# Windowed attention and SwiGLU on one core: the second token group loaded in token order

## The chip, the cores and the metric

The kernel runs on one core of a Trainium2 chip. The core has five engines that run side by side: TensorE (matrix products; weight loads and products are listed apart as PEld and PE), VectorE (DVE), ScalarE (ACT), GpSimd (POOL) and SyncE (SP). Data come from HBM by DMA, over 16 transfer engines that all queues share. The metric is the device time of one execution in microseconds (us), median of several.

## The reference

It is an attention over a sliding window with sink tokens, followed by a gated feed-forward block. There are 4 sequences of 768 tokens, 8 heads of 64.

```python
scores = scale * np.matmul(q, k.transpose(0, 1, 3, 2))
is_sink = pos[None, :] < n_sink                  # 4 sink tokens
rel = pos[:, None] - pos[None, :]
in_window = (rel >= 0) & (rel < window)          # window of 128
scores = np.where(is_sink | in_window, scores, -1e9)
a = np.exp(scores - scores.max(-1, keepdims=True))
a = a / (a.sum(-1, keepdims=True) + 1e-09)
attn = np.matmul(a, v)
# ... heads side by side: x is (3072, 512)
g = x @ w_gate                                   # 512 x 1536
val = x @ w_val
out = (g * sigmoid(g) * val) @ w_out             # 1536 x 512
```

## The kernel before: the parts that matter

The tokens are cut into 12 groups of 256 (3 to a sequence). For each group the kernel loads k, q and v, turns k and q so that the head dimension lies on the partitions, computes scores, exponentials, masks, values and normalization, turns the result (xn) into xT, and hands it to the gate, value and down projections. These are slices of matmuls ("units") in whose gaps the attention of later groups is woven. The order on every engine is the order of the program.

Group 0 is loaded first, in a form of its own. Group 1 is loaded by rows: each partition gets four tokens of one head in one piece of 256 numbers, and 64 small matmuls against an identity turn it. Groups 2 and 3 are loaded in token order (a partition is a token, its heads are pieces of 64 numbers) and turned by full 128x128 transposes.

```python
def load_rows(g, i):                       # i: k or q; two issues, one per half of the heads
    for w in range(2):
        nc.gpsimd.dma_start(rows[g][64 * w:64 * (w + 1), i],
                            by_rows((k, q)[i], b, w, ALL, c * 256))

def load_nat(g):                           # token order; k and q, two issues each
    # ...
    for i, src in ((0, k), (1, q)):
        for j in range(2):
            nc.gpsimd.dma_start(x[:, i, j].rearrange("p (h d) -> p h d", d=D),
                                src[b, :, t0:t0 + P].rearrange("h p d -> p h d"))

def step_T(g, i, p2, evict=None):          # turns rows: 16 matmuls of 64x64 and a copy
    # ...
def step_TN(g, i, j, evict="av"):          # turns token order: 4 transposes of 128x128
    pt = bank([P, NP2, P], BF16, "pn")
    for p in range(NP2):
        nc.tensor.transpose(pt[:, p], nats[g][:, i, j, p * P:(p + 1) * P], ident)
    # ... one copy out of PSUM, on ScalarE ("a") or VectorE ("v")
```

The loads on GpSimd's queue come in this order at the start: k and q of group 0 (heads 4 to 7; the others go over other queues), k and q of group 1, v of group 0, gate piece 0 (w_gate and w_val, 256 columns each), v of group 1, gate pieces 1 and 2; then group 2 and further weights.

The opening after group 0's scores:

```python
fill(14, bank([P, 512], FP32, "w"))        # matmuls on zeros, 256 columns, at the very start
# ... group 0: casts, turning, scores, masks
step_T(1, 0, 0, "a")
step_T(1, 0, 1, "a")
step_ks(0)                                 # the sinks' keys
step_T(1, 1, 0, "a")
step_T(1, 1, 1, "a")
step_PV(0, 0, 0)                           # values of group 0: (group, token half, head half)
step_PV(0, 0, 1)
flush()                                    # VectorE: normalization that was put off
step_PV(0, 1, 0)
step_PV(0, 1, 1)
flush()
step_S(1, 0)                               # scores of group 1, heads 0 to 3
masks1 = list(later)
later.clear()
step_K(1)                                  # scores against the sinks
step_X(0, 0, "now")                        # xn of group 0 turned into xT
step_X(0, 1, "now")
step_S(1, 1)                               # scores of group 1, heads 4 to 7
later[:0] = masks1
flush()
```

After it come the units. The first holds gate and value slices 0 and 1 of group 0 (`gate_held`); then `gate_first` computes the values of group 1 and starts gate slices 2 and 3, which need gate piece 1:

```python
us = [(gate_held, *g0[0][1:]), (gate_first, *g0[1][1:]), g1[0], g1[1], g0[2], g1[2],
      *((gate, "01", f) for f in range(6, DFC)),   # groups 0 and 1 joined: 512 columns
      *g2, *downs(0), *downs(1), *downs(2)]

def gate_first(tb, f, attn):
    for j, hh, norm in ((0, 0, "v"), (1, 0, "v"), (0, 1, "a"), (1, 1, "v")):
        step_PV(1, j, hh, norm)            # norm: "a" scales on ScalarE, "v" on VectorE
        flush()
    a = gate_a(tb, f)
    step_X(1, 0, "a")                      # copy on ScalarE
    step_X(1, 1, "now")                    # copy on VectorE
    held.pop()()
    gate_b(tb, f, *a)
```

A unit of one group, such as `g0[2]`, does two slices of the hidden dimension for 256 tokens; a joined unit ("01") does one slice for 512 tokens.

Of the kernel before, what the change touches and what calls it, by code (L numbers as in the profile page):

```python
# [7 lines left out]
FP32 = mybir.dt.float32  # L8
BF16 = mybir.dt.bfloat16
# [5 lines left out]
def kernel(  # L15
# [62 lines left out]
    def bank(shape, dtype, name):  # L78
        return psum.tile(shape, dtype, tag="b", name=name)


    rows, nats, vas = {}, {}, {}

    def by_rows(src, b, w, pairs, t0):

        hs = slice(2 * pairs.start + w, 2 * pairs.stop, 2)
        return src[b, hs, t0:t0 + 256].rearrange("p (m r) d -> m p (r d)", r=4)

    ALL = slice(0, NP2)

    def new_rows(g):
        rows[g] = rowp.tile([P, 2, NP2, 4 * D], BF16, tag="rows", name="rows")
        return rows[g]

    def load_rows(g, i):
        b, c = divmod(g, GC)
        if g not in rows:
            new_rows(g)
        for w in range(2):
            nc.gpsimd.dma_start(  # L100
                rows[g][64 * w:64 * (w + 1), i],
                by_rows((k, q)[i], b, w, ALL, c * 256))

    def load_nat(g):
        b, c = divmod(g, GC)
        x = (natp if g > 3 else rowp).tile(
            [P, 2, 2, DM], BF16, tag="nat" if g > 3 else "rows", name="nat")
        for i, src in ((0, k), (1, q)):
            for j in range(2):
                t0 = c * 256 + j * P  # L110
                nc.gpsimd.dma_start(  # L111
                    x[:, i, j].rearrange("p (h d) -> p h d", d=D),
                    src[b, :, t0:t0 + P].rearrange("h p d -> p h d"))
        nats[g] = x
# [37 lines left out]
    th8 = const.tile([P, 4, 4], FP32)  # L152
    lt8 = const.tile([P, 4, 4], FP32)
    sk = const.tile([P, 1], FP32)
    zero = const.tile([P, 256], BF16)
    one = const.tile([P, 1], FP32)
    warmed = const.tile([P, 1], FP32)
    KW = 32
# [28 lines left out]
    for i in range(2):  # L187
# [2 lines left out]
                   allow_small_or_imprecise_dtypes=True)  # L190
    nc.gpsimd.iota(tk, [[0, 1]], base=0, channel_multiplier=1,
                   allow_small_or_imprecise_dtypes=True)
    load_rows(1, 0)
    load_rows(1, 1)
    load_v(0)
    nc.gpsimd.iota(th8, [[-32, 4], [-NS, 4]], base=0, channel_multiplier=1,
                   allow_small_or_imprecise_dtypes=True)
# [12 lines left out]
    def flush():  # L210
        for f in later:
            f()
        later.clear()

    def new_T(b):
        if b not in kTs:
            kTs[b] = kqtp.tile([P, NP2, S], BF16, tag="kT", name="kT")
            qTs[b] = kqtp.tile([P, NP2, S], BF16, tag="qT", name="qT")

    def step_T(g, i, p2, evict=None):  # L220
        b, c = divmod(g, GC)
        new_T(b)
        x = rows[g]
        pt = bank([P, 2, 256], FP32, "pt")
        for pp in range(2):
            p = 2 * p2 + pp
            for r in range(4):
                for w in range(2):
                    h = slice(64 * w, 64 * (w + 1))
                    nc.tensor.matmul(  # L230
                        pt[h, pp, r:256:4], x[h, i, p, r * D:(r + 1) * D],
                        ident[h, h], start=True, stop=True, skip_group_check=True)
        dst = (kTs, qTs)[i][b][:, 2 * p2:2 * p2 + 2, c * 256:(c + 1) * 256]
        if (evict or ("a", "v")[i]) == "a":
            nc.scalar.copy(out=dst, in_=pt)
        else:
            nc.vector.tensor_copy(out=dst, in_=pt)

    def step_TN(g, i, j, evict="av"):

# [67 lines left out]
    def step_K(g):  # L308
        b, c = divmod(g, GC)
        if c == 0:  # L310
            return
        ps = bank([P, P], FP32, "pk")
        kfl = kss.rearrange("q b p x -> q b (p x)")
        for a in range(2):
            for j in range(2):
                for hh in range(2):
                    r, p = 32 * (2 * j + hh), 2 * hh + a
                    t0 = c * 256 + j * P
                    k0 = (KW + 2 * NS) * p - 2 * NS * a
                    nc.tensor.matmul(  # L320
                        ps[r:r + KW], kfl[:, b, k0:k0 + KW], qTs[b][:, p, t0:t0 + P],
                        start=(a == 0), stop=(a == 1), skip_group_check=True)
        es_t[g] = espool.tile([P, P], BF16, tag="es", name="es")
        nc.scalar.activation(es_t[g], ps, AF.Exp, scale=scale)
# [54 lines left out]
    def step_X(g, j, evict="v"):  # L379
        t0 = g * 256 + j * P  # L380
        tb = max(i for i in range(len(SIZES)) if OFF[i] <= t0)
        off = t0 - OFF[tb]
        if tb == 0 and off == 0:
            xTs["01"] = xtp.tile([P, DMC, 512], BF16, tag="xT", name="xT")
            xTs[0], xTs[1] = (xTs["01"][:, :, 256 * i:256 * (i + 1)] for i in range(2))
        elif tb > 1 and off == 0:
            xTs[tb] = dense(xtp.tile([P, DMC * 512], BF16, tag="xT", name="xT"),
                            DMC, SIZES[tb])
        if g not in PEX:
            def sp():  # L390
                nc.sync.dma_start_transpose(xTs[tb][:, :, off:off + P], xns[g, j])
            later.append(sp)
            return
        pt = bank([P, DMC, P], BF16, "px")
        for i in range(DMC):
            nc.tensor.transpose(pt[:, i], xns[g, j][:, i * P:(i + 1) * P], ident)  # L396

        if evict == "a":
            nc.scalar.copy(out=xTs[tb][:, :, off:off + P], in_=pt)
            return  # L400

        def dve():
            nc.vector.tensor_copy(out=xTs[tb][:, :, off:off + P], in_=pt)
        if evict == "now":
            dve()
        else:
            later.append(dve)
# [59 lines left out]

    def gate_first(tb, f, attn):

        for j, hh, norm in ((0, 0, "v"), (1, 0, "v"), (0, 1, "a"), (1, 1, "v")):  # L470
            step_PV(1, j, hh, norm)
            flush()
        a = gate_a(tb, f)
        step_X(1, 0, "a")
        step_X(1, 1, "now")
        held.pop()()
        gate_b(tb, f, *a)
# [62 lines left out]
    def fill(n, ps, cols=256):  # L540
        for _ in range(n):
            nc.tensor.matmul(ps[:, 0:cols], zero[:, 0:P], zero[:, 0:cols], start=True,
                             stop=True, skip_group_check=True)
# [40 lines left out]
        m = mask0.rearrange("q (o a) x -> q o (a x)", o=1)[:, :, P:512]  # L584
        nc.vector.tensor_tensor(e, e, m.broadcast_to([P, 2, 384]), op=ALU.mult)

    fill(14, bank([P, 512], FP32, "w"))
    cast(0, 0)
    cast(1, 0)
    nc.vector.tensor_scalar(mask[:, :, 0:P], tq2, tk, None, op0=ALU.is_lt)  # L590
# [28 lines left out]
    for i in range(4):  # L619
# [4 lines left out]
    nc.gpsimd.memset(vcl[:, :, D:D + 1], 1.0)  # L624
    load_sinks(vcl, 1, B)

    step_T(1, 0, 0, "a")
    step_T(1, 0, 1, "a")
    step_ks(0)
    step_T(1, 1, 0, "a")  # L630
    step_T(1, 1, 1, "a")
    step_PV(0, 0, 0)
    step_PV(0, 0, 1)
    flush()
    step_PV(0, 1, 0)
    step_PV(0, 1, 1)
    flush()
    step_S(1, 0)
    masks1 = list(later)
    later.clear()  # L640
    step_K(1)
    step_X(0, 0, "now")
    step_X(0, 1, "now")
    step_S(1, 1)
    later[:0] = masks1
    flush()

    g0, g1, g2 = gates(0), gates(1), gates(2)
    us = [(gate_held, *g0[0][1:]), (gate_first, *g0[1][1:]), g1[0], g1[1], g0[2], g1[2],
          *((gate, "01", f) for f in range(6, DFC)),  # L650
          *g2, *downs(0), *downs(1), *downs(2)]

    def L(*fs):
# [76 lines left out]
```

## Time and profile before

| what | value |
|---|---|
| time, median of 3 | 238.78 us (238.61 to 238.98) |
| span of the profiled execution | 237.8 us |
| TensorE busy | 229.1 us, 96% of the span |
| VectorE, ScalarE, GpSimd busy | 158.4, 113.7, 74.5 us |
| TensorE clock granted | full in every slice |
| gate and value matmuls (pg, pv) | 73.1 us each |
| down matmuls (pd) | 64.8 us |
| data moved by DMA | 27.36 MB in 107,655 packets |

The page gives busy time by engine; the chain that ended last tells what released what, back from the end; a timeline lists the instructions of an engine in order, with its idle time before them and what ended it in brackets. In the names, `pg<-xT,wg` is a matmul that writes tile pg from xT and the weights wg. L417 is the line of both projections, L100 the row loads, L122 the loads of v, L133 those of w_gate and w_val.

### The profile page before, as it was taken

The page shows a single profiled execution, that of the slowest core. Times are in us where ns is not written, and L with a number is a line of the kernel's source. Part 1 is how long each engine was busy: PE and PEld are TensorE (multiplying, and loading weights), DVE is VectorE, ACT ScalarE, POOL GpSimd, SP SyncE. Part 2 cuts the span into 40 slices and gives each one's busy share as a digit, 9 for nine tenths or more (in the row PEclk, how much of TensorE's full clock was granted, in tenths as well). Part 3 has the DMA queues.
Part 4 walks back from the last instruction along what each step waited for, and adds up shares of the span by engine and source line. Part 5 has one row for each costly group of instructions (what it writes and reads, how often), then busy time and mean ns, then how long its engine had stood idle before and what let it go on. Part 6 is the DMA issues. An engine that isn't in the chain of part 4 may idle for free.

```text
span 237.8 us, 4880 instructions
## 1 busy us (share of the span) xinstructions
PE 229.1 (96%) x1874; PEld 127.5 (54%) x1901; DVE 158.4 (67%) x336; ACT 113.7 (48%) x233; POOL 74.5 (31%) x98
## 2 busy tenths in 40 slices
PE   8889999999999999999999999999999999999994
PEld 4558945795554444444444444445454445488443
DVE  5887888768652898970788980588970598877000
ACT  4884485467452845512745622655622663333221
POOL 8977775730808017070260800080000000000000
PEclk9999999999999999999999999999999999999999
DMA  8999999994999979999499994599204100200132
GB/s 139 153 179 178 180 199 205 159 146 73 129 142 171 187 127 110 138 128 225 112 126 103 105 87 139 137 100 140 44 17 137 70 3 0 44 3 0 51 129 88
DMA packets 107655, 27.36 MB, mean 115 GB/s; under 512 B 94704, under 2 KB 104688, under 8 KB 107632
## 3 DMA queue, kind: packets, MB, share of 16 engines
q0 software_dynamic: 76640, 13.90, 76.7%
q1 hardware_dynamic: 30448, 12.89, 25.3%
q8 instruction: 15, 0.25, 0.4%
q10 hardware_dynamic: 544, 0.26, 0.4%
q14 instruction: 8, 0.07, 0.1%
HBM read 28.34 MB, written 6.29 MB: 146 GB/s over the span
## 4 chain that ended last, share of the span: by engine, by line
PE 84%; DMA 6%; POOL 4%; DVE 2%; issue 2%; ACT 1%; SPq 0%; POOLq 0%; DVEq 0%; ACTq 0%
PE pv L417 26%; PE pg L417 25%; PE pd L492 22%; PE s L292 4%; PE o L355 4%; DMA wg<-in_moe_w_gate_dram 4%; DMA xT<-xn 3%; POOL va L122 1%; POOL rows L100 1%; PE pn L245 1%; POOL x L188 1%; PE o L335 1%; PE pk L320 1%; ACT th L437 1%; PE px L396 1%
## 5 line engine op out<-in xcount | busy, mean ns | idle before, releaser
L417 PE MATMUL pg<-xT,wg 128*128 128x512 bf16 (+1 forms) x351 | 73.1, 335 | 1.9 <-DMA wg<-in_moe_w_gate_dram 1.1
L445 DVE SCALAR_TENSOR_TENSOR u<-th,pg 128x512 bf16<-128x512 f32 x72 | 49.1, 682 | 38.3 <-ACT th L437 38.3
L417 PE MATMUL pv<-xT,wv 128*128 128x512 bf16 (+1 forms) x351 | 73.1, 336 | 0.5 <-ACT e L299 0.2
L437 ACT ACTIVATE th<-pg 128x512 f32<-128x512 f32 x72 | 43.5, 604 | 62.9 <-PE pg L417 59.2
L492 PE MATMUL pd<-wo,ht 128*128 128x512 bf16 (+2 forms) x291 | 64.8, 370 | 0.4
L451 DVE TENSOR_TENSOR ht<-u,pv 128x512 bf16<-128x512 bf16 x66 | 45.4, 687 | 9.8 <-PE pv L417 2.9
L417 PEld LDWEIGHTS <-wg 128*128 128x128 bf16 x360 | 35.0, 98 | 29.6 <-DMA wg<-in_moe_w_gate_dram 1.5
L299 ACT ACTIVATE e<-s 128x512 bf16<-128x512 f32 (+1 forms) x88 | 42.9, 581 | 4.3 <-PE s L292 4.3
L492 PEld LDWEIGHTS <-ht 128*128 128x128 bf16 x300 | 27.9, 98 | 29.9 <-issue 0.5
L417 PEld LDWEIGHTS <-wv 128*128 128x128 bf16 x360 | 32.1, 98 | 20.5 <-issue 1.7
L111 POOL DMA_DIRECT2D nat<-in_k_dram x20 | 17.6, 886 | 76.8 <-DMA qT<-nat 73.2
L497 ACT ACTIVATE ot<-pd 128x512 f32<-128x512 f32 (+1 forms) x24 | 14.3, 596 | 47.4 <-PE pd L492 43.4
L304 DVE TENSOR_TENSOR e<-e,mask 128x1024 bf16<-128x1024 bf16 (+1 forms) x44 | 27.1, 649 | 4.1 <-ACT e L299 4.1
L122 POOL DMA_DIRECT2D va<-in_v_dram x24 | 21.5, 918 | 4.0 <-DMA wo<-in_moe_w_out_dram 2.5
L369 DVE TENSOR_TENSOR xn<-o,rcp 128x256 bf16<-128x256 f32 x45 | 19.1, 424 | 1.5
L355 PEld LDWEIGHTS <-e 128*128 128x128 bf16 x352 | 15.1, 98 | 7.8 <-issue 0.3
L111 POOL DMA_DIRECT2D nat<-in_q_dram x20 | 17.7, 896 | 1.0 <-DMA wg<-in_moe_w_gate_dram 0.5
L355 PE MATMUL o<-va,e 128*128 128x65 bf16 x352 | 17.1, 193 | 0.3 <-DMA va<-in_v_dram 0.2
L292 PE MATMUL s<-qT,kT 64*128 64x128 bf16 (+1 forms) x240 | 13.0, 237 | 0.0
L292 PEld LDWEIGHTS <-kT 64*128 64x128 bf16 x240 | 7.7, 94 | 7.6 <-issue 6.6
L363 DVE RECIPROCAL rcp<-o 128x4 f32<-128x4 f32 x48 | 8.2, 174 | 2.5 <-PE o L355 2.5
L499 DVE TENSOR_SCALAR ot<-pd 128x128 f32<-128x128 f32 x1 | 0.3, 290 | 14.3 <-PE pd L492 14.3
(73 smaller groups left out, 91.1 us busy)
## 6 DMA issues: line engine op xcount, KB each, us to landing
out_dram<-ot SPq DMA_DIRECT2D x23, 256.0 KB
va<-in_v_dram POOLq DMA_DIRECT2D x24, 128.0 KB, 6.5
nat<-in_k_dram POOLq DMA_DIRECT2D x20, 128.0 KB, 4.4
nat<-in_q_dram POOLq DMA_DIRECT2D x20, 128.0 KB, 5.7
wg<-in_moe_w_gate_dram POOLq DMA_DIRECT2D x6, 256.0 KB, 8.5
wv<-in_moe_w_val_dram POOLq DMA_DIRECT2D x6, 256.0 KB, 8.8
wo<-in_moe_w_out_dram POOLq DMA_DIRECT2D x4, 384.0 KB, 11.1
st<-in_q_dram ACTq DMA_DIRECT2D x2, 128.0 KB
```

What stands on the lines that cost most here:

```text
L111: nc.gpsimd.dma_start(x[:, i, j].rearrange("p (h d) -> p h d", d=D), src[b, :, t0:t0 + P].rearrange("h p d -> p h d"))
L122: nc.gpsimd.dma_start(va[:, j, :, 0:D], v[b, :, t0:t0 + P].rearrange("h p d -> p h d"))
L292: nc.tensor.matmul(pss[2 * pp + h][:, col:col + n], kTs[b][r, p, kk:kk + P], qTs[b][r, p, qq:qq + n], start=True, stop=True)
L299: nc.scalar.activation(e_t[g][:, h0 + h, lo:512], pss[2 * pp + h][:, lo:512], AF.Exp, scale=scale)
L304: nc.vector.tensor_tensor(e, e, m[:, :, lo:512].broadcast_to([P, 2, 512 - lo]), op=ALU.mult)
L355: nc.tensor.matmul(o, l, r, start=(c == 0 and i == 0), stop=(i == len(mms) - 1), skip_group_check=True)
L369: nc.vector.tensor_tensor(xn, po[:, :, 0:D], rcp.broadcast_to([P, 4, D]), op=ALU.mult)
L417: nc.tensor.matmul(ps[:, i * n:(i + 1) * n], ws[fi][:, c, fo * P:(fo + 1) * P], xTs[tb][:, c], start=(c == 0), stop=(c == DMC - 1))
L437: nc.scalar.activation(th, pg, AF.Tanh, scale=0.5)
L445: nc.vector.scalar_tensor_tensor(u, th, 1.0, pg, op0=ALU.add, op1=ALU.mult)
L451: nc.vector.tensor_tensor(hts[tb][:, f:f + 512 // SIZES[tb]].rearrange("p a n -> p (a n)"), u, pv, op=ALU.mult)
L492: nc.tensor.matmul(po, hts[tb][:, f, ts * P:(ts + 1) * P], wos[f // n][:, f % n, lo:hi], start=(f == 0), stop=(f == DFC - 1))
```

## The change

Group 1 gets the load and the turning of groups 2 and 3; the code for row loads goes. The filler matmuls at the very start have 512 columns instead of 256, and half the count. The first scores of group 1 are computed between the two halves of group 0's values, so that ScalarE has exponentials earlier. In `gate_first` ScalarE normalizes the first and the last block of values instead of the third, and VectorE copies both halves of xT. The units of groups 0 and 1 are joined from slice 4 on (the fifth) instead of slice 6.

```diff
-    def load_rows(g, i): ...
-    def step_T(g, i, p2, evict=None): ...
...
-    zero = const.tile([P, 256], BF16)
+    zero = const.tile([P, 512], BF16)
...
-    load_rows(1, 0)
-    load_rows(1, 1)
+    load_nat(1)
     load_v(0)
...
-        for j, hh, norm in ((0, 0, "v"), (1, 0, "v"), (0, 1, "a"), (1, 1, "v")):
+        for j, hh, norm in ((0, 0, "a"), (1, 0, "v"), (0, 1, "v"), (1, 1, "a")):
             step_PV(1, j, hh, norm)
             flush()
         a = gate_a(tb, f)
-        step_X(1, 0, "a")
+        step_X(1, 0, "now")
         step_X(1, 1, "now")
...
-    fill(14, bank([P, 512], FP32, "w"))
+    fill(7, bank([P, 512], FP32, "w"), 512)
...
-    step_T(1, 0, 0, "a")
-    step_T(1, 0, 1, "a")
+    step_TN(1, 0, 0, "aa")
+    step_TN(1, 0, 1, "aa")
     step_ks(0)
-    step_T(1, 1, 0, "a")
-    step_T(1, 1, 1, "a")
+    step_TN(1, 1, 0, "aa")
+    step_TN(1, 1, 1, "aa")
     step_PV(0, 0, 0)
     step_PV(0, 0, 1)
-    flush()
-    step_PV(0, 1, 0)
-    step_PV(0, 1, 1)
     flush()
     step_S(1, 0)
     masks1 = list(later)
     later.clear()
+    step_PV(0, 1, 0)
+    step_PV(0, 1, 1)
     step_K(1)
-    step_X(0, 0, "now")
+    step_X(0, 0)
+    flush()
     step_X(0, 1, "now")
     step_S(1, 1)
...
-    us = [(gate_held, *g0[0][1:]), (gate_first, *g0[1][1:]), g1[0], g1[1], g0[2], g1[2],
-          *((gate, "01", f) for f in range(6, DFC)),
+    us = [(gate_held, *g0[0][1:]), (gate_first, *g0[1][1:]), g1[0], g1[1],
+          *((gate, "01", f) for f in range(4, DFC)),
```

More of the change, by code (lines that the diff above doesn't have):

```diff
@@ L79, in bank @@
         return psum.tile(shape, dtype, tag="b", name=name)
[L82 to L102, printed above, removed]
+    nats, vas = {}, {}
     def load_nat(g):
@@ L218, in new_T @@
             qTs[b] = kqtp.tile([P, NP2, S], BF16, tag="qT", name="qT")
[L220 to L237, printed above, removed]
     def step_TN(g, i, j, evict="av"):
```

## The prediction

> **What bounds the kernel now.** I read the page's busy row first, then the chain that ended last over the opening microseconds, then the timeline of TensorE and of GpSimd there, and last the raw records of the transfers. The busy row and the DMA row of the page:
>
> ```profile
> PE 229.1 (96%) x1874; PEld 127.5 (54%) x1901; DVE 158.4 (67%) x336; ACT 113.7 (48%) x233; POOL 74.5 (31%) x98
> ...
> DMA  8999999994999979999499994599204100200132
> ```
>
> TensorE is busy in 229.1 of 237.8 us, and the transfer engines are at nine tenths through the first nine slices (some 53 us). So there is little slack, and what there is lies at the start and in the last 3.5 us, which the change does not touch. The chain from 8 to 24 us:
>
> ```profile
> 9.17 1.64 POOL va L122 x2
> 10.81 8.63 DMA wg<-in_moe_w_gate_dram
> 19.44 0.05 issue
> 19.48 1.05 PE pg L417 x8
> 20.53 0.52 PE px L396 x8
> 21.05 0.87 PE pv L417 x8
> 21.92 0.87 PE pg L417 x8
> 22.80 0.87 PE pv L417 x8
> ```
>
> See in it that until 19.44 us the end is set by a load: the second piece of w_gate, issued at 10.81, which must have been loaded before the second gate slice. From 19.48 on it is TensorE without a gap. So the time is "when the second gate slice starts" plus a dense stretch. What TensorE does just before that:
>
> ```profile
> 15.77 1.05 PE L417 MATMUL pg<-xT,wg 128*128 128x256 bf16 x8 [0.69 <-DMA wg<-in_moe_w_gate_dram]
> 16.65 1.04 PE L417 MATMUL pv<-xT,wv 128*128 128x256 bf16 x8
> 17.62 0.29 PE L335 MATMUL o<-vsb,es 32*128 32x260 bf16 x4
> 17.84 1.20 PE L355 MATMUL o<-va,e 128*128 128x65 bf16 x32
> 19.48 1.05 PE L417 MATMUL pg<-xT,wg 128*128 128x256 bf16 x8 [0.44 <-DMA wg<-in_moe_w_gate_dram]
> ```
>
> The brackets show two waits on weights, 0.69 us for the first piece and 0.44 us for the second. The values of group 1 end at 19.04, so only 0.44 us of the start is the load's alone: speeding the load up by more than that gains nothing unless the attention work before it is earlier too.
>
> Then GpSimd, which issues all these loads:
>
> ```profile
> 3.23 1.28 POOL L100 DMA_DIRECT2D rows<-in_k_dram  x2
> 4.47 1.27 POOL L100 DMA_DIRECT2D rows<-in_q_dram  x2
> 5.67 1.86 POOL L122 DMA_DIRECT2D va<-in_v_dram  x2
> ```
>
> Two row issues take some 1.24 us from start to start, two token-order issues (v has the layout that k and q will get) 1.8 us. In the raw records a row load is 256 packets of 512 bytes at 60 to 65 ns each; a token-order load is 1024 packets of 128 bytes at 32 ns each. In saturated stretches the engines finish some 370 of the first or 1150 of the second per us: 0.69 us for a row load, 0.89 us for a token-order one.
>
> One more thing in the raw records: each load marks its semaphore 16 times[...]. Of the second w_gate piece, 15 marks were there at 17.81 us and the last only at 19.44. The same single laggard shows in the first piece (13.44, last 15.72), so it began about 13 us. The only unusual transfer there is this one, from the DMA view of 13 to 15 us:
>
> ```profile
> q0 software_dynamic: 1636, 0.33, 190.8%
> q8 instruction: 1, 0.02, 3.0%
> ```
>
> It is one packet of 16384 bytes at 13.66 us that took 0.945 us. Over the run there are 15 of them, and TensorE has 3,804 instructions, 254 to a packet. I read it as the fetch of TensorE's next instructions, sitting on one transfer engine in the midst of its share of weights and setting the wait that the chain shows. At that moment 358 of TensorE's recorded instructions had started.
>
> [...]
>
> **The change part by part.**
>
> Loads. Four issues grow by (1.8 - 1.24)/2 = 0.28 us each, so GpSimd issues everything behind them 1.1 us later. On the transfer engines they grow from a saturated 4 x 0.69 = 2.8 us to 4 x 0.89 = 3.6, that is +0.8. But before, these engines weren't saturated there: the row packets went through at 264 and 237 per us at 6 and 7 us, and all 1024 took from about 5.7 to 9.3. The token-order ones, fed at 0.9 us per issue and needing 0.89, take as long. So I expect the weights later by 0.2 to 0.8 us, 0.3 most likely.
>
> Turning group 1. 64 matmuls in two bursts of 1.08 us go, 16 transposes come (8 took 0.45 us in the chain where group 2 is turned). The last of them starts when the last q load lands: 10.44 us before, some 10.75 after; then 4 transposes, about 0.25, and one ScalarE copy of 0.55, to 11.6. Before, two copies ended at 12.22. So group 1's scores can start 0.6 us earlier; they now stand between group 0's values, so that they start at about 12.1 instead of 12.65 us and the exponentials at 12.4 instead of 13.08.
>
> Group 0's other two value blocks move behind these scores: from 12.1 to about 12.6 us. Their normalization on VectorE (0.17 + 0.42 us twice) ends at 14.2, the copies of xT (2 x 0.45) at 15.1 instead of 14.92. The second half of the scores follows at 14.6 to 15.2 (before 14.38 to 15.07), its exponentials end at 17.1 (17.27), the masks at 17.8 (17.99).
>
> First gate. Without the laggard the first piece lands at 13.44 + 0.3, so gate and value slice run from xT at 15.2 to 17.0, with no wait, and group 1's values from 17.1 to 18.5 instead of 19.04. Hence the second gate slice could start at 18.6 instead of 19.48 us: -0.9 us.
>
> Instruction fetch. Up to that point the new program has 14 (filler) + 96 (turning) = 110 TensorE instructions fewer. The 358th is now what was the 468th, in the second half of group 1's values, at about 18.0 to 18.8 us. The second w_gate piece has then landed (17.81 + 0.3 = 18.1), but the second w_val piece (15 marks at 19.13, +0.3) may still be moving; if the fetch hits it, it lands at 19.4 + 1.6 = 21.0. Its matmuls would be due at 18.6 + 0.87 + 0.52 = 20.0 and then start at 21.0 against 21.05 before: gain nil.
>
> Normalization of group 1 (ScalarE takes the first and last block, VectorE both copies): ScalarE's four small scalings took 0.93 us, so the last end about 19.9, and the last transpose of group 1's xn waits perhaps 0.2 us. Cost 0.1 to 0.2.
>
> Filler. 14 matmuls of 256 columns or 7 of 512: the same columns, 3.1 us; clearing the wider tile adds 0.1 us on VectorE. Nothing on the path.
>
> Joined units. Two units of 256 columns (4 x 0.87 = 3.48 us) become two of 512 (4 x 0.86 = 3.44): -0.04 us. Same VectorE and ScalarE work, same eight banks.
>
> Sum: -0.9 + 0.15 - 0.04, about -0.8 us if the fetch misses the weights; about 0 if it hits the second w_val piece.
>
> **The rivals.** (a) The loads take over: 0.8 to 1.1 us later with the laggard still in front of the second w_gate piece, because the fetch comes earlier than I count. For it: transfers bind the start in the chain. Then +0.3 to +0.8, 239.1 to 239.6. (b) The fetch moves behind both pieces: -0.8, 238.0. For it: the 110 instructions; against it: the w_val piece is still moving then. (c) The fetch hits w_val: the wait at the second gate turns into a wait one group later; 238.7 to 238.9. (d) VectorE becomes the bound: the copies of xT wait behind two more normalizations and delay the second half of the scores, so that group 1's values start later. It had 0.0 to 0.3 us gaps from 12 to 18 us, so it is close; +0.3.
>
> **Range and chances.** I give (a) 25%, (b) 30%, (c) 35%, (d) 10%: 0.25 x 239.3 + 0.30 x 238.0 + 0.35 x 238.8 + 0.10 x 239.1 = 238.7; I lean a little to the earlier scores and say 238.5. The three times before span 0.37 us. Range 237.7 to 239.5. Two per cent is 4.8 us; nothing here moves more than 1.2, so within 2% has 98%, and either side 1%.
>
> **What would show it.** The chain should still come from a load into TensorE at 18.6 to 20.1 us, and from there run as before, the remainder the same to 0.2 us. GpSimd's issue of the second w_gate piece should start near 11.9 us. The exponentials of group 1 should start before 12.8. The 16384-byte packet should come after 17.5 us and the laggard with it. I am wrong if group 1's scores start later than 12.65 (the load of q is then worse than I think), if the dense part changes by over 0.5 us (the joined units then do something that I do not see), or if VectorE stands in the chain before the second gate slice.

## The result and the profile after

| | before | after |
|---|---|---|
| time, median of 6 executions each, taken side by side | 238.97 us (238.61 to 239.65) | 240.76 us (239.98 to 241.45) |
| ratio after to before, 95% interval | | 1.0069 (1.0041 to 1.0097) |
| the same, taken a second time (52 and 17 executions) | 238.83 us | 239.60 us, 1.0032 (1.0022 to 1.0042) |
| span of the profiled execution | 237.8 us | 239.1 us |

The change makes the kernel slower by 0.3 to 0.7%. The prediction was 238.5 us with a range of 237.7 to 239.5. The profiles are of one execution each, and that of before is of a late one: it took 239.56 us, 0.7 us above the median of the 52. First the page of the changed kernel: its busy row, and the row of the granted clock over 40 slices of 6 us.

```profile
PE 231.0 (97%) x1830; PEld 125.0 (52%) x1830; DVE 159.8 (67%) x336; ACT 114.2 (48%) x236; POOL 75.5 (32%) x98
...
PEclk9979999999999999999999999999999999999999
```

The digit 7 in the third slice of PEclk is what is new: there the clock was below full. It was full in every slice before. (The busy time, 231.0 against 229.1 us, can't be compared to a microsecond: the page of before has 1874 matmuls to 1901 weight loads, so records are missing; the profile of a kernel with the same matmuls and all 1901 records has 230.8 us, and a second one of the changed kernel, with a mean clock of 1.000, has 230.1.) Next the windows of the changed kernel around that slice; the columns are the window, its length, busy us of PE, PEld, DVE, ACT and POOL (with counts), the granted clock, and the transfers.

```profile
8.42:11.83 3.41, 2.12 (x30) 1.39 (x28) 3.11 (x10) 3.37 (x10) 3.41 (x6) 1.00 2.17 149
11.83:15.25 3.42, 3.28 (x48) 2.42 (x44) 2.36 (x9) 2.65 (x6) 3.31 (x6) 0.50 1.67 173
```

For 3.42 us TensorE ran at half rate (in the raw records the matmuls of group 0's values start 29 ns apart just ahead of it, 54 to 57 in it), right after a stretch of the same length in which it was busy for 2.12 us. A half rate over 3.42 us lowers the mean over 239.1 us to 1 - 0.5 x 3.42 / 239.1 = 0.993, the mean clock of this execution. So the mean clock of any execution tells whether it had such a dip: of the 23 executions of the changed kernel 11 had one (0.991 to 0.993), the other 12 none (0.998 to 1.000).

The chain that ended last, changed kernel, around the second gate slice (start, us, what):

```profile
18.19 0.60 PE o L315 x16
...
19.04 0.42 DVE xn L329
...
19.59 0.42 DVE xn L329
...
20.14 0.94 ACT xn L326 x4
...
21.12 0.23 PE px L356
21.35 0.87 PE pv L377 x8
```

No load stands here any more. Group 1's values are followed by two normalizations on VectorE and one on ScalarE, and only then by the second value slice at 21.35 us, where the chain of before had it at 21.05. The timeline of TensorE shows the same from the engine's side:

```profile
16.07 1.03 PE L377 MATMUL pg<-xT,wg 128*128 128x256 bf16 x8
...
19.11 1.04 PE L377 MATMUL pg<-xT,wg 128*128 128x256 bf16 x8
...
20.71 0.23 PE L356 MATMUL px<-ident,xn 128*128 128x128 bf16 x1 [0.23 <-ACT xn L326]
21.12 0.23 PE L356 MATMUL px<-ident,xn 128*128 128x128 bf16 x1 [0.18 <-ACT xn L326]
21.19 1.04 PE L377 MATMUL pv<-xT,wv 128*128 128x256 bf16 x8
```

Both gate slices start without a bracket, so without a wait for weights, and the second is 0.37 us earlier than the 19.48 of before's profile. Then two waits for ScalarE's xn (0.23 and 0.18 us) use this up: the value slice starts at 21.19, against 20.89 in the timeline of before.

From there the two traces keep a distance of +0.27 us up to 76 us, +0.08 after it, and +1.26 after 112 us. What happens at 112 us, in the chain of the changed kernel:

```profile
105.89 7.45 DMA xT<-xn
113.33 0.04 issue
113.38 1.02 PE pg L377 x4
```

and in that of the kernel before:

```profile
105.79 6.28 DMA xT<-xn
112.07 0.04 issue
112.12 1.02 PE pg L417 x4
```

Later groups have xn turned into xT not by TensorE but by DMA transposes that SyncE issues. The one for the second half of group 6 was issued 0.1 us later and took 1.17 us longer. TensorE waited 1.22 us for it. What was on the transfer engines meanwhile, from GpSimd's timeline of the changed kernel:

```profile
101.55 1.75 POOL L91 DMA_DIRECT2D nat<-in_k_dram  x2 [8.41 <-DMA qT<-nat]
103.28 1.77 POOL L91 DMA_DIRECT2D nat<-in_q_dram  x2
105.00 1.79 POOL L102 DMA_DIRECT2D va<-in_v_dram  x2
```

These six loads belong to group 8. The kernel before issued the first of them at 100.48, here at 101.55: they lie just ahead of the transpose. So three things stand beside each other in this trace: the dip, the later start, and the wait for xT.

### The profile page after: what moved, and what is told of

The parts are those of the page before. It is cut to its first block, busy times and chain, and to the rows that moved or that the text cites. A ratio compares the mean times of both kernels' runs of the same rounds, so it can differ in the third digit from the quotient of the medians.

```text
span 239.1 us, 4769 instructions
## 1 busy us (share of the span) xinstructions
PE 231.0 (97%) x1830; PEld 125.0 (52%) x1830; DVE 159.8 (67%) x336; ACT 114.2 (48%) x236; POOL 75.5 (32%) x98
## 4 chain that ended last, share of the span: by engine, by line
PE 88%; DMA 3%; ACT 3%; DVE 3%; issue 1%; SPq 0%; DVEq 0%; ACTq 0%
PE pv L377 26%; PE pg L377 26%; PE pd L452 22%; PE s L252 5%; PE o L315 4%; DMA xT<-xn 3%; PE w L502 1%; DVE xn L329 1%; PE px L356 1%; PE pt L518 1%; PE pn L205 1%; PE o L295 1%; PE pk L280 1%; ACT th L397 1%; ACT e L539 1%
## 5 line engine op out<-in xcount | busy, mean ns | idle before, releaser
L377 PE MATMUL pg<-xT,wg 128*128 128x512 bf16 (+1 forms) x352 | 74.1, 340 | 1.4 <-DMA xT<-xn 1.2
L377 PE MATMUL pv<-xT,wv 128*128 128x512 bf16 (+1 forms) x352 | 74.2, 341 | 0.3 <-ACT e L259 0.2
L452 PE MATMUL pd<-wo,ht 128*128 128x512 bf16 (+2 forms) x300 | 65.7, 371 | 0.0
L411 DVE TENSOR_TENSOR ht<-u,pv 128x512 bf16<-128x512 bf16 x64 | 44.0, 688 | 9.6 <-PE pv L377 3.9
L377 PEld LDWEIGHTS <-wg 128*128 128x128 bf16 x352 | 34.2, 98 | 30.1 <-issue 2.5
L91 POOL DMA_DIRECT2D nat<-in_k_dram x22 | 19.4, 889 | 77.9 <-DMA qT<-nat 75.2
L377 PEld LDWEIGHTS <-wv 128*128 128x128 bf16 x352 | 31.4, 98 | 20.9 <-issue 1.7
L91 POOL DMA_DIRECT2D nat<-in_q_dram x22 | 19.5, 898 | 1.6 <-DMA wv<-in_moe_w_val_dram 1.0
L252 PE MATMUL s<-qT,kT 64*128 64x128 bf16 (+1 forms) x240 | 13.5, 242 | 0.1
```

Of the source, the lines that this page charges most:

```text
L252: nc.tensor.matmul(pss[2 * pp + h][:, col:col + n], kTs[b][r, p, kk:kk + P], qTs[b][r, p, qq:qq + n], start=True, stop=True)
L377: nc.tensor.matmul(ps[:, i * n:(i + 1) * n], ws[fi][:, c, fo * P:(fo + 1) * P], xTs[tb][:, c], start=(c == 0), stop=(c == DMC - 1))
L411: nc.vector.tensor_tensor(hts[tb][:, f:f + 512 // SIZES[tb]].rearrange("p a n -> p (a n)"), u, pv, op=ALU.mult)
L452: nc.tensor.matmul(po, hts[tb][:, f, ts * P:(ts + 1) * P], wos[f // n][:, f % n, lo:hi], start=(f == 0), stop=(f == DFC - 1))
```

## The experiments

A ratio is to executions of the kernel before on the same chip (medians 238.8 to 238.9), with its 95% interval. "Dip" means a mean clock of 0.993 or less.

**One part at a time.** The first four kernels separate the token order, the joined units, the changed opening without token order, and TensorE's idleness.

Kernel before with `load_nat(1)` and `step_TN` for group 1, and nothing else:

```diff
-    load_rows(1, 0)
-    load_rows(1, 1)
+    load_nat(1)
...
-    step_T(1, 0, 0, "a")      # and the three others
+    step_TN(1, 0, 0, "aa")
```

> The kernel before with only the token-order load and the 16 transposes of group 1. Theory (the transposes leave TensorE too idle between 8.4 and 11.8 us, so its clock is halved for 3.4 us): a granted clock below 1.000 in most executions, the dip at about 12 us, and in those the start later by 0.3 to 1 us than without. Rival (the clock dip comes from the wide filler matmuls or from the new order): clock 1.000 throughout, time within 0.3 us of before. If the wait for xT at 112 us comes from the token-order load, this kernel shows it too (1.2 us on TensorE); otherwise TensorE waits there under 0.2 us.

Measured: 239.48 us, 1.0036 (1.0020 to 1.0052), 19 executions, 5 with a dip. The 14 others have a median of 239.28. So the dip comes with the token order alone, but in fewer executions than expected. In the profile (no dip) TensorE runs 0.45 us ahead of before's profile from 23 us on, and loses this lead at 76 us. The token order costs time even without the rest of the change.

Kernel before with the joined units alone:

```diff
-    us = [..., g1[0], g1[1], g0[2], g1[2], *((gate, "01", f) for f in range(6, DFC)),
+    us = [..., g1[0], g1[1], *((gate, "01", f) for f in range(4, DFC)),
```

> The kernel before with only the units of groups 0 and 1 joined from slice 4. Theory: no effect of its own at the start, time within 0.3 us of before, clock 1.000. Rival[...]: the wait for xT at 112 us appears or changes by over 0.5 us with the start unchanged.

Measured: 242.54 us in 4 executions, 1.0167 (1.0131 to 1.0204), 3 of them with a dip; not explained by anything the edit does. The profiled execution (240.29, no dip) again ran 0.45 us ahead, and then waited 1.40 us for xT. Its chain at that place:

```profile
70.54 6.25 DMA xT<-xn
76.80 0.14 issue
76.93 1.02 PE pg L417 x4
```

and its loads of the next group, on GpSimd:

```profile
70.31 1.76 POOL L111 DMA_DIRECT2D nat<-in_k_dram  x2 [7.73 <-DMA qT<-nat]
```

The kernel before issued these loads after the transposes:

```profile
72.50 1.75 POOL L111 DMA_DIRECT2D nat<-in_k_dram  x2 [7.75 <-DMA qT<-nat]
```

Here they come 0.23 us ahead of the last one, which takes 6.25 us. This is the first sight of the pattern: an earlier start lets the next loads go in front of the transpose.

The changed kernel with group 1 loaded and turned by rows, as before, all else kept:

```diff
-    load_nat(1)
+    load_rows(1, 0)
+    load_rows(1, 1)
...
-    step_TN(1, 0, 0, "aa")     # and the three others
+    step_T(1, 0, 0, "a")
```

> The changed kernel with group 1 loaded and turned by rows as before, everything else as changed. Theory (token order makes the clock dip): clock 1.000 in all executions, and the start not later than before plus 0.3. Rival (wide filler or new order make it): the dip stays in most executions. For the wait for xT at 112 us: if it stays at about 1.2 us, it isn't the token-order load that makes it.

Measured: 238.99 us, 1.0015 (0.9998 to 1.0032), 20 executions without a single dip. They form two clusters, 12 at 238.5 to 239.4 and 8 at 239.8 to 240.6. The profiled one (240.20) is of the upper cluster, and waits for xT, as TensorE's timeline shows:

```profile
76.88 0.81 PE L417 MATMUL pg<-xT,wg 128*128 128x512 bf16 x3 [1.26 <-DMA xT<-xn]
```

The distance of the clusters is about this wait. Without token order the dips are gone; the wait is not.

The changed kernel with six matmuls on zeros (512 columns) around the transposes of group 1's q:

```diff
+    warm = bank([P, 512], FP32, "w")
+    fill(2, warm, 512)
     step_TN(1, 1, 0, "aa")
+    fill(2, warm, 512)
     step_TN(1, 1, 1, "aa")
+    fill(2, warm, 512)
```

> The changed kernel with six more matmuls on zeros (512 columns) in the waits between group 1's transposes and after them, 1.3 us of TensorE at full clock. Theory (the dip comes from an idle TensorE at 8.4 to 11.8 us): clock 1.000 in all executions, the scores of group 1 and what follows to 15 us at full speed, and the median 0.5 to 1 us below the changed kernel's. Rival (transposes or the load are not the cause): the dip stays and the time is the same or longer. The wait for xT at 112 us is expected to stay.

Measured: 239.35 us, 1.0030 (1.0015 to 1.0045), 20 executions, no dip; again two clusters (12 up to 239.47, 8 from 239.99). Work that computes nothing takes the dips away. The time is 1.4 us below the first median of the changed kernel, but only 0.25 us below the second. The work also occupies TensorE, and the kernel is not faster than before.

**Is it the normalization?** The changed kernel with the old division of work in `gate_first`:

```diff
-        for j, hh, norm in ((0, 0, "a"), (1, 0, "v"), (0, 1, "v"), (1, 1, "a")):
+        for j, hh, norm in ((0, 0, "v"), (1, 0, "v"), (0, 1, "a"), (1, 1, "v")):
...
-        step_X(1, 0, "now")
+        step_X(1, 0, "a")
```

> The changed kernel with group 1's normalizations and copies divided as before (ScalarE the third block and the first copy). Theory (the last transpose of group 1's xn waits for ScalarE's scalings of the last block, two gaps of 0.18 and 0.23 us in the trace of the changed kernel): the second value slice starts 0.4 us earlier, 20.7 instead of 21.19 us in the trace; the median falls by 0 to 0.4 us, since a later wait for xT can take it back. The clock dip stays in some executions. Rival (ScalarE is no bound, the gap is the load): no change at the start.

Measured: 239.86 us, 1.0042 (1.0026 to 1.0058), 19 executions, 11 with a dip. The second value slice started at 21.48 us, not at the 20.7 expected, and the waits for ScalarE's xn stayed at 0.4 us in sum. No support for the normalization as the cause.

**Is it the loads in front of the transposes?** A tiny copy on GpSimd that reads the last column of xT makes GpSimd wait for the transpose; the loads of groups 6 and 8 are put behind such a copy, which waits for the last transpose of group 3 and of group 6. First with the changed kernel:

```diff
+    seen = const.tile([P, 1], BF16)
+    def landed(tb, off):
+        nc.gpsimd.tensor_copy(out=seen, in_=xTs[tb][:, DMC - 1, off + P - 1:off + P])
...
-        (19, [A(xbar, 5)]), (19, [NV(6)]),
+        (19, [A(xbar, 5)]), (21, [A(landed, 3, 128), NV(6)]),
...
-        (2, [A(xbar, 7)]), (2, [NV(8)]),
-        ... *pair(5, 6),
+        (2, [A(xbar, 7)]),
+        ... *pair(5, 6), (14, [A(landed, 4, 384), NV(8)]),
```

> The changed kernel; GpSimd issues the loads of groups 6 and 8 only when the transposes of xn of groups 3 and 6 have landed (a tiny copy on GpSimd reads their last column first). Theory (those loads, 6 x 0.9 us on all transfer engines, lie in the way of the transposes that the gates wait for at 76 and 112 us): the transposes land in about 3 us instead of 4 to 7, TensorE waits under 0.2 us at both places, and the median falls by 0.5 to 1.2 us; the spread of the executions narrows to the clock dip alone. Rival (the transposes are slow by themselves, or through the output stores): waits and time unchanged.

Measured: 239.81 us, 1.0028 (1.0016 to 1.0040), 20 executions, 15 with a dip (median 239.86), 5 without (median 238.72). The wait for xT is gone from the profile. SyncE issues the last transpose at 105.20:

```profile
105.20 1.24 SPq L351 DMA_TRANSPOSE xT<-xn  x1
```

and GpSimd's timeline shows it landed before the copy, and the loads after it:

```profile
107.74 0.19 POOL L626 COPY seen<-xT 128x1 bf16<-128x1 bf16 x1 [15.62 <-DMA xT<-xn]
108.81 1.76 POOL L91 DMA_DIRECT2D nat<-in_k_dram  x2 [0.88 <-DMA out_dram<-ot]
```

With none of these loads ahead of it the transpose landed at 107.62 (its 16th mark in the raw records), in 2.4 us instead of 7.45. Executions without a dip are now 0.8 us faster than such executions of the changed kernel (238.72 against 239.51 in a later run of 17, below), so the waits cost about that much; and with the waits gone a dip costs 239.86 - 238.72 = 1.1 us in full. As 15 of 20 had a dip, the median of all shows nothing of it.

The same hold in the kernel before:

> The kernel before with the same two loads held back. Theory (before had no wait there to lose, it just fitted): time within 0.4 us of before, the transposes land some us earlier relative to their issue. Rival (the loads needed to be early): the next groups' transposes come late and the time rises by over 0.5 us.

Measured: 238.60 us, 0.9991 (0.9980 to 1.0001), 20 executions, no dip. The kernel before had little of this to lose, 0.2 us, and the interval allows nothing at all. Its profile served for one thing more. Its opening is that of the kernel before to the letter, yet the gate slices start like this:

```profile
15.15 1.05 PE L417 MATMUL pg<-xT,wg 128*128 128x256 bf16 x8
...
18.64 1.05 PE L417 MATMUL pg<-xT,wg 128*128 128x256 bf16 x8
```

Neither has the wait for weights (0.69 and 0.44 us) that the prediction started from. The raw records of the transfers, beside it (times in us at which the 15th and 16th of a load's marks came):

```
                  first w_gate piece   second w_gate piece   16384-byte packet
before              13.44   15.72        17.81   19.44         13.66, 0.945 us
before, held        13.47   13.51        17.89   18.60         13.51, 0.948 us
after               14.02   14.50        18.53   18.87         15.84, 0.939 us
```

The packet came at nearly the same time (13.51 against 13.66) and took as long, and the last mark of the first piece was 0.04 us behind the 15th, not 2.28. The lag differs from execution to execution of the same opening. Whether the packet makes part of it stays open: the next load of the held kernel, the first w_val piece, has its 15th mark at 14.81 and its last at 15.75, and 0.94 us is the length of the packet; but in a further kernel of these experiments (rows, with the hold) the packet came at 13.14 and the same load was only 0.09 us apart (13.95 and 14.04).

**What makes the dip?** All three of the following have the hold.

The changed kernel with the six idle-time matmuls and the old normalization:

> The changed kernel with the six matmuls on zeros, the normalizations as before, and both loads held back. If the three causes (clock dip, ScalarE's last block, loads in the way of the transposes) are all there is: clock 1.000, span near 236.5 us, median about 238.3, that is 0.3 to 0.7 us below before, with a spread under 1 us. If it stays above before, a fourth cause is missing.

Measured: 239.05 us, 1.0006 (0.9994 to 1.0019), 12 executions, no dip, and one cluster only, 0.9 us wide. With dips and waits removed the changed kernel equals the kernel before, but doesn't beat it: the 238.3 expected was missed, and the kernel before with the same hold is at 238.60. So something in the change, or the zero matmuls, still costs time.

Group 1 turned by ordinary matmuls against the identity, into fp32, instead of transposes:

```diff
+    def step_TM(g, i, j):
+        # ...
+        pt = bank([P, NP2, P], FP32, "pm")
+        for p in range(NP2):
+            nc.tensor.matmul(pt[:, p], nats[g][:, i, j, p * P:(p + 1) * P], ident,
+                             start=True, stop=True, skip_group_check=True)
+        # ... one copy on ScalarE
...
-    step_TN(1, 0, 0, "aa")     # and the three others
+    step_TM(1, 0, 0)
```

> The changed kernel with both loads held back, and group 1 turned by the same 16 products against the identity issued as ordinary matmuls into float32 PSUM instead of transposes. Theory A[...]: no execution with a clock near 0.993, median 238.7 as in the undisturbed executions of the kernel with loads held back. Theory B (TensorE is just too idle from 8.4 to 11.8 us, whatever the sort of instruction): the dip in about 15 of 20 executions as with transposes, median 239.8.

Measured: 239.51 us, 1.0022 (1.0009 to 1.0034), 20 executions, 10 with a dip (median 239.88, without 238.71). The windows of its profile:

```profile
10.97:14.38 3.41, 2.01 (x45) 1.56 (x46) 2.16 (x12) 2.96 (x9) 3.41 (x6) 1.00 1.38 162
14.38:17.80 3.42, 3.33 (x29) 2.12 (x28) 3.20 (x8) 2.85 (x8) 3.29 (x6) 0.50 1.88 179
```

The dip is there without a transpose. So it isn't the kind of instruction that makes it. That it has to do with how little TensorE does is shown by the zero matmuls: no dip in 20 and 12 executions with them. In this trace and in that of the changed kernel the half rate lasts equally long, 3.41 to 3.42 us at 0.50, but begins at a different time (14.38 and 11.83 us). TensorE was not idle throughout ahead of it: the windows before the dips of four traces were busy for 1.82 to 2.12 us of 3.41. There were 10 dips in 20 executions of matmuls against 15 in 20 of transposes; whether the kind of instruction adds to it these numbers don't settle.

The filler at the start back to 14 matmuls of 256 columns:

```diff
-    fill(7, bank([P, 512], FP32, "w"), 512)
+    fill(14, bank([P, 512], FP32, "w"))
```

> The changed kernel with both loads held back and the filler of before (14 matmuls of 256 columns). Theory (filler has nothing to do with the dip): dips in about 15 of 20 executions, median 239.8. Rival[...]: dips in under a third of the executions, median below 239.2.

Measured: 239.71 us, 1.0025 (1.0010 to 1.0041), 20 executions, 11 with a dip, those without at 238.71. The filler is not the cause: it may be narrow or wide.

For comparison, traces without a dip. In the clock record of the changed kernel full rate begins at 5.01 us and lasts 6.83 us, then comes half rate for 3.41 and full rate for 225.28: 2, 1 and 66 times 3.413. In that of the kernel before, full rate lasts from 4.00 us for 235.52, 69 times 3.413; ahead of it, where there is no record, its matmuls of 256 columns started 213 ns apart, in the first gate slice 109. So the openings of these traces too were cut into windows of 3.41 us from the clock's first rise to full rate (between 3.9 and 7.1 us in the 15 traces that record it); shown is the one with the least, or nearly the least, TensorE work of each. The kernel before:

```profile
7.41:10.82 3.41, 2.73 (x60) 1.76 (x58) 3.30 (x11) 2.86 (x8) 3.41 (x7) 1.00 1.75 155
```

The token order alone:

```profile
9.33:12.74 3.41, 2.20 (x44) 1.74 (x43) 3.18 (x12) 3.21 (x9) 3.41 (x6) 1.00 1.92 160
```

The changed kernel with the hold:

```profile
8.12:11.53 3.41, 2.41 (x34) 1.59 (x31) 3.31 (x11) 3.21 (x9) 3.41 (x6) 1.00 2.24 147
```

In the four traces with a dip TensorE was busy for 1.82 to 2.12 us of the 3.41 before it, in these three for 2.20 or more in every window of the opening, and in the eight other traces with a record of the clock and no dip for 2.33 or more. Where the windows begin matters for what they hold: the changed kernel's fell at 8.42 us and held 2.12, the held one's at 8.12 and held 2.41. Laid at the worst place of the opening, such a window holds 1.73 to 2.00 us of work in the six traces with both the token order and the new order of scores and values, 2.20 and 2.33 in the two with the token order alone, and 2.50 or more in the nine with rows or with the zero matmuls. The counts go the same way: 58 of 102 executions, 11 of 39 and, but for the kernels with joined units alone and one execution of the kernel before, none. Row loading has 64 small matmuls where token order has 16 transposes. TensorE doesn't need the work of the 64 for the result, but with these two exceptions the dips came only where it was gone and no zero matmuls stood in its place.

Recorded busy time alone doesn't decide, though. The kernel with joined units alone had a window of 2.07 us while it waited for xT, and no dip behind it:

```profile
75.59:79.00 3.41, 2.07 (x26) 1.03 (x27) 0.38 (x1) 1.60 (x4) 0.00 (x0) 1.00 1.60 270
79.00:82.41 3.41, 3.41 (x22) 1.44 (x21) 2.88 (x6) 2.29 (x7) 0.00 (x0) 1.00 1.97 159
```

**A version that beats both.** The changed kernel with group 1 loaded by rows, and with the hold:

> The changed kernel with group 1 loaded and turned by rows as before, and both loads held back. Theory: no dip, no wait for xT, so that whatever order, filler, normalization and joined units are worth by themselves is seen: median 238.2 to 238.7, against 238.6 of before with loads held back. If it is above 238.9 the rest of the change costs time by itself.

Measured: 238.47 us, 0.9982 (0.9970 to 0.9993), 20 executions from 237.86 to 238.87, no dip. Its gate and value slices in TensorE's timeline:

```profile
18.06 1.03 PE L417 MATMUL pg<-xT,wg 128*128 128x256 bf16 x8
...
19.66 0.23 PE L396 MATMUL px<-ident,xn 128*128 128x128 bf16 x1 [0.23 <-ACT xn L366]
20.07 0.23 PE L396 MATMUL px<-ident,xn 128*128 128x128 bf16 x1 [0.18 <-ACT xn L366]
20.14 1.04 PE L417 MATMUL pv<-xT,wv 128*128 128x256 bf16 x8
```

The value slice is 0.75 us ahead of the 20.89 of before's profile, and here the end is 1.18 us earlier. But that profile is of a late execution. The kernel with joined units alone, taken again (below), has the opening of before, no hold and no wait, and in its profile the value slice starts at

```profile
20.29 1.04 PE L417 MATMUL pv<-xT,wv 128*128 128x256 bf16 x8
```

and the end is 1.03 us earlier. What is shown is that the change without the token order, with the hold, beats the kernel before and the changed one. That the new order of scores and values has a part in it is not shown: the kernel before with the hold alone had 0.9991 (0.9980 to 1.0001), and the intervals overlap.

**Repeats and remainders.** The joined units alone, once more:

> The kernel before with only the joined units once more, because its clock was at 0.993 in 3 of 4 executions although its opening is that of before. Theory (chance, or a disturbance of that session): under a fifth of executions at 0.993, median 238.6 to 239.4, with a second cluster about 1.2 us higher from the wait for xT at 76 us. Rival (joined units make a second dip): most executions at 0.993 and above 242 us.

Measured: 239.32 us, 1.0020 (0.9999 to 1.0040), 12 executions; one at 242.12 was left out of the ratio as disturbed, and it alone had a low clock. Apart from it the 242.5 of the first four did not come again; eight lie at 238.2 to 239.4 and three at 239.8 to 240.7, like the two clusters above. What made the first four slow stays open. An estimate from the figures above: the profiled execution, with its wait of 1.40 us, took 240.29, and half rate for 3.41 us where TensorE has no gap costs 1.7 more, so 242.0; a dip behind that wait would come near the three slow ones, but none of them was profiled.

The changed kernel once more:

> The changed kernel itself, in the same session as the next two, for more executions of it. Theory (clock dip in most executions, 1.1 us each; the wait for xT at 76 or 112 us in some, about 1.2 us each): four clusters near 238.7, 239.8, 240.0 and 241.1 us, median 240 to 240.8, at least half of the executions near clock 0.993.

Measured: 239.60 us, 1.0032 (1.0022 to 1.0042), 17 executions, 7 with a dip (median 239.91), 10 without (239.51). So the expectation of 240 or more was missed; here a dip adds 0.4 us only. That without the hold part of a delay at 15 us is made up by a shorter wait at 76 or 112 us would explain it, but is not shown; in the first six executions the four with a dip were 1.1 us above the two without (241.09 and 240.00). Why those six were slower, dip or no dip, stays open.

The token order alone, with the hold:

> The kernel before with only the token-order load and turning of group 1, and both loads held back. Theory (the idle of TensorE in the turning makes the dip; the new order of scores and values makes it more likely): dips in 15 to 40% of the executions, undisturbed ones at 238.3 to 238.7, median 238.6 to 239. Rival (the order has no part in it): dips in over half, median above 239.3.

Measured: 238.99 us, 1.0017 (1.0001 to 1.0033), 20 executions, 6 with a dip (median 239.98), 14 without (238.89). Two of the six, at 241.1 us, have a mean clock of 0.986, that of two dips. Against the held kernel before, 238.60, the token order costs some 0.3 us with neither dip nor wait, and more than the 238.7 expected. The dips are fewer than the 15 of 20 of the whole change with the hold, though not than the 7 of 17 of the changed kernel on this same chip; it is the counts together (11 of 39 against 58 of 102) and the windows above that say the new order of scores and values adds to them.

The version that beats both, with the old normalization:

> The changed kernel with group 1 by rows, both loads held back, and group 1's normalizations divided as before. Theory (ScalarE's last block delays the last transpose of group 1's xn by 0.4 us, and nothing takes the gain back now): median 238.0 to 238.3, against 238.47 without this. Rival (the second w_gate or w_val piece lands just behind anyway): no difference.

Measured: 238.62 us, 0.9984 (0.9975 to 0.9994), 20 executions, no dip. No gain over 238.47. Its chain shows why:

```profile
18.11 0.42 DVE xn L369
...
18.66 0.43 DVE xn L369
...
19.21 0.94 ACT xn L366 x4
...
20.19 0.45 PE px L396 x5
```

The third block goes to ScalarE instead of the fourth, but it is still two normalizations of VectorE and then ScalarE's 0.94 us that the value slice waits for. The kernel with joined units alone, taken again, has the same two waits in the opening of before (0.21 and 0.18 us): there too ScalarE's block ends last when no load is late.

## Why the prediction was wrong

It expected the kernel to be 0.3 us faster, and it was 0.8 to 1.8 us slower. By its own steps:

- **"From there run as before, the remainder the same to 0.2 us": this step failed.** The time was to be the start of the second gate slice plus a dense stretch. The stretch isn't rigid, and it had no unbroken chain of TensorE work even before: the 6.28 us of DMA at 105.79 stand in the chain of before. At 76 and 112 us TensorE meets a DMA transpose whose landing depends on whether the next group's loads go ahead of it, and it took 2.4, 6.3 or 7.45 us. In the profiled executions the two places made +1.0 us of the +1.3 (-0.2 at 76, +1.2 at 112). Over many executions without a dip, the hold takes 0.8 us from the changed kernel (239.51 to 238.72) and 0.2 from the kernel before. Gains at the start of the first trials (-0.45, -0.45, -0.37) ended at this point as well.
- **The clock of TensorE was no step at all.** Turning group 1 with 16 instructions instead of 64 was booked as pure gain. It leaves TensorE at 1.8 to 2.1 busy us of 3.41, and in about half of the executions the next 3.41 us run at half rate: +1.1 us where nothing hides it, +0.4 in the larger sample of the changed kernel as it stands. The zero matmuls remove it, ordinary matmuls instead of transposes don't.
- **First gate, -0.9 us: the time was right, the gain was not.** In the two profiles of the changed opening without a dip the second gate slice starts at 18.57 and 18.83 us; 18.6 was predicted. But the 19.48 that it was set against belongs to one late execution: in three other profiles with the opening of before it starts at 18.24, 18.64 and 18.89. So this term was worth about nothing. A wait seen in one execution was taken for the kernel's.
- **Turning group 1, 0.6 us earlier: failed.** The prediction counted the last transpose and one ScalarE copy, to 11.6 us. ScalarE had two copies of qT to do after other work, and they end where they ended before, at 12.25 (before 12.22). After the change:

```profile
11.18 1.07 ACT L209 COPY qT<-pn 128x512 bf16<-128x512 bf16 x2
```

and before it:

```profile
11.15 1.07 ACT L235 CAST qT<-pt 128x512 bf16<-128x512 f32 x2
```

- **Scores at 12.1, exponentials at 12.4: half right.** The first scores were issued at 11.87, on the first of the two copies; the exponentials came at 12.81 (13.08 before). The dip isn't why: in the held kernel's profile, without one, they came at 12.67.
- **Instruction fetch: failed.** The packet came at 15.84, not at 18.0 to 18.8. Counting started instructions was no way to place it: 358 of TensorE's recorded instructions had started at the packet of before, 279 at this one. That it holds TensorE's instructions was the author's reading of the queue's name, instruction, and of 15 packets to 3,804 instructions (the changed kernel has 14 packets); no trace shows what is in it. And the packet wasn't shown to make the lag of 1.63 us. What makes the last mark late stays open.
- **Loads +0.2 to +0.8, 0.3 most likely: right.** The 15th mark of the second w_gate piece moved from 17.81 to 18.53, +0.7, in the upper half. GpSimd's issue of it came at 11.85 (11.9 predicted).
- **Normalization 0.1 to 0.2: not shown.** The waits for ScalarE are 0.4 us in this trace (0.23 + 0.18), and they took the place of the load at the end of the chain. But the old division has them too (0.21 + 0.18), and giving it back didn't help in either kernel. So the division isn't what costs; the chain of VectorE and ScalarE behind group 1's values is.
- **Filler and joined units, about nothing: right for the filler,** 238.71 without a dip with either. The joined units alone gave 1.0020 (0.9999 to 1.0040), no gain that shows.

Of the rivals, (a), the loads taking over, gave 239.1 to 239.6; the second median of 239.60 lies at its edge, but for other reasons. That VectorE would stand in the chain was rival (d) at 10%. It does, one step later than named, between the second gate and the second value slice; in the opening of before it stands there as well when no load is late.

The account in numbers, without dips: 239.51 - 238.83 = 0.7 us for the change. The hold brings the two kernels to 238.72 and 238.60, so some 0.6 of this is waits for xT. What is left is about as small as the medians can tell, as they come from several chips: for the token order 0.25 us (238.72 against 238.47 with rows) or 0.3 (238.89 against 238.60), and for the new opening a gain of 0.13 at most (238.60 to 238.47), which isn't resolved. The dips come on top. Which of the two held places matters more was not tried apart.

## What to carry to other kernels

A start that comes earlier is worth something only if the transfers further on don't hand it back: before counting a gain at the start, look for every later transpose or load that lands just in time, and ask which queue will get ahead of it. Before replacing many small matmuls by few large ones where TensorE waits for data anyway, add up its busy time over each 3.4 us: in the openings here 2.12 us (62%) was followed by half rate and 2.20 (64%) wasn't, so a stretch in that region may lose its clock, and the saving with it. Before counting a shorter turning as gain, look at the engine that copies its result. And a wait seen in one profile of one execution should be seen in a second before a prediction is built on it.

## What the runs showed of the hardware that was not expected

- In the opening TensorE fell to half rate for one stretch of 3.41 to 3.42 us after a stretch of that length with 1.82 to 2.12 us of recorded work; 2.20 us or more had no such effect there. In the changed kernel's trace no single idle gap of that stretch was over 0.54 us. Recorded work alone doesn't decide: at 75.59 us of another trace 2.07 us had no such effect. Of the kernels with the token order and no zero matmuls, each had it in some executions and not in others, from 5 of 19 to 15 of 20. In the clock record of the changed kernel the stretches after the first rise to full rate are 6.83, 3.41 and 225.28 us long, in that of the kernel before 235.52, all whole multiples of 3.413; the first rise came between 3.9 and 7.1 us.
- A DMA transpose issued by SyncE, of 2.4 us when GpSimd's loads were held back, took 6.25 to 7.45 us in three traces where six loads from GpSimd's queue, another than its own, were issued around it.
- The last of the 16 marks of a load, the first w_gate piece, came 0.01 to 2.28 us behind the 15th in four executions with the same program up to there.
